# Smaller stages for the weight preparation at the seam between two stages of a fused attention and feed-forward kernel

## The chip, the cores and the metric

One core of one Trainium2 chip runs the whole kernel. The metric is device microseconds (us) of one execution; the kernel before took 1059.97 us (median of three runs, 1059.31 to 1060.24). The engines are PE (matmuls and weight loads), DVE (vector), ACT (scalar), POOL (GpSimd) and SP, whose queue issues the DMAs. Each engine works through its own list of instructions in order; semaphores hold an instruction until its inputs are there.

## The reference

Attention over 4 x 8 heads of 576 tokens and 64 dimensions, with scores below the row's maximum minus `tau` masked out, and then two feed-forward layers over the 2304 tokens:

```python
x = attention(q, k, v, tau)          # [2304, 512]
h = ((x @ w1) * (x @ w2)) @ w3       # gated, d_ff 1024
h3 = h @ w_out                       # [2304, 512]
g = h3 @ w_in                        # second layer, d_ff 2048
out = np.maximum(0.01 * g, g) @ w2_out
```

All of it is wanted in float32 accuracy; the weights arrive as 64-bit numbers.

## The kernel before

**Numbers.** A float32 matrix is held as a high part that PE can take (`fp32r`) and a low part, the rest; a product is then three matmuls (high x high, high x low, low x high, the table `PASSES`). The 64-bit weights come from HBM as pairs of 32-bit words into a tile `st`. `words` turns one `st` into two integer tiles `t` and `lw` with two ACT conversions (L640, L641) and a DVE shift of `t` (L642); a POOL addition of `t` and `lw` makes the float32 (L657 for up weights, L691 for down weights). `t` and `lw` have two buffers each, `st` has four.

**Stages.** Attention runs first, with the gated layer of each group of tokens as filler between its steps (`gated`: eight parts i; each has 24 `psab` matmuls on PE (L439), a copy `at` on ACT (L445), the product of the two halves on DVE (L447), a cast of `gt` to its high part on ACT (L449) and a subtraction for the low part on POOL (L450). Four outputs o follow, each of 24 `psh` matmuls (L458) that take the eight `gt` in order, a copy `ht` (L465) and a store to `h3d`). The gated layer of the last group has no attention left beside it: it is the chain `last`, walked step by step. Beside it run `first_h3`, which builds the operands `h3` of the second layer, and the first weight preparations; the table `early` says at which steps.

**The second layer** takes the tokens in three chunks of 768 and d_ff in eight quadruples (`NQ`), so 24 products n. `products(n)` is seven blocks of six matmuls (L854; a scheme with seven products of half-size blocks) into two banks of PSUM in turn; each block's bank is freed by a copy `snap` on ACT (L831), a `sum` on DVE (L836) or the activation `gf` on ACT (L841). `down(n)` is 36 `po` matmuls (L889); five follow each block of the next product and six the last.

**The preparations.** `prepare_up(q)` makes the seven combinations of quadruple q (`full`: one L664 and three L711 on DVE), their high parts `uph` (two ACT casts of 768 and 1024 columns, L671) and low parts `upl` (two DVE subtractions, L674), and stores both to `up_d` (L677) for the later chunks. `prepare_down(q)` makes `dn`: per half a cast (L690) and a subtraction (L711), then a store to `dn_d` (L695). In the first chunk, product n calls one step of `prepare_up(n + 2)` per block and, from block 3, one of `prepare_down(n + 1)`; what is left runs after block 6. `fetch` brings a quadruple's tiles back in the later chunks; for three of eight they are still in place. `load_h3` prepares the next chunk's operands during the last product of a chunk. ACT, DVE and POOL take their instructions in the order in which the code issues them (`manual_schedule`); so does PE.

Of the kernel before, what the change touches and what calls it, by code (L numbers as in the profile page):

```python
# [43 lines left out]
def attention_gated_ffn(ctx: ExitStack, tc: tile.TileContext, qkv, tau, w3t, wout, w12, w2, out):  # L44
# [576 lines left out]
    ups = [[(q + NQ, 0), (q, 0)] for q in range(NQ)] + [[], []]  # L621
    downs = [[(q, 1), (q + NQ, 1)] for q in range(NQ)]
    order = ups[0] + downs[0] + ups[1] + [x for q in range(1, NQ + 1) for x in ups[q + 1] + downs[q % NQ]][:-2]
# [9 lines left out]
    def words(j, c):  # L633
# [7 lines left out]
        nc.scalar.activation(lw, low.bitcast(U32), AF.Copy, scale=2.0 ** -29)  # L641
        nc.vector.tensor_scalar(out=t, in0=t, scalar1=3, scalar2=None, op0=ALU.logical_shift_left)  # L642
        used[0] += 1
        return t, lw

    def prepare_up(q):
# [3 lines left out]

        full = wpool.tile([P, 8, HF], F32, tag=tag(q), name="full")
        uph, upl = up_tiles(q)
        kept = None
        for j, part in ((q + NQ, full[:, 0:2]), (q, full[:, 2:4]), (None, None)):
            if kept:
                into, t, lw = kept
                nc.gpsimd.tensor_tensor(  # L657
                    out=into.rearrange("p a w -> p (a w)").bitcast(I32), in0=t, in1=lw, op=ALU.add)
            if j is not None:
                kept = (part, *words(j, 0))  # L660
                issue()
            yield
# [7 lines left out]
        for lo, hi in parts:  # L670
            nc.scalar.copy(uph[:, lo:hi], full[:, 1 + lo:1 + hi])  # L671
        yield
# [3 lines left out]
        for i, part in enumerate((uph, upl)):  # L676
            nc.sync.dma_start(out=up_d[q, i], in_=f(part.rearrange("p a w -> p (a w)")))  # L677
        yield

    def prepare_down(q):  # L680

        dn = down_tile(q)
        kept, low = None, None
        for i in range(4):
            if low is not None:
                less(dn[:, i - 2, 1], f(low), f(dn[:, i - 2, 0]))
                low = None
            if kept:
                t, low = kept
                nc.scalar.copy(dn[:, i - 1, 0], f(t))  # L690
                nc.gpsimd.tensor_tensor(out=low, in0=t, in1=low, op=ALU.add)  # L691
            kept = words(q + i * NQ, 1) if i < 2 else None
            issue()
            if i == 3:
                nc.sync.dma_start(out=dn_d[q], in_=f(dn.rearrange("p a b w -> p (a b w)")))  # L695
            yield
# [276 lines left out]
```

## Time and profile before

| | |
|---|---|
| median of three runs | 1059.97 us |
| profiled execution | 1061.28 us, span 1059.5 us |
| PE busy | 1027.7 us (97%) |
| DVE, ACT, POOL busy | 582.3, 547.2, 282.5 us |
| chain that ended last, by engine | PE 90%, ACT 4%, DVE 3%, POOL 1%, issue 1% |
| mean granted clock of PE | 0.987 |

The times of a row are of one profiled execution, whose own time stands above; its span runs from the first to the last instruction. A row of an engine's timeline gives start, duration, line, operation, output and inputs, the number of instructions merged into it, and in brackets the idle time before it with what ended that. The granted clock of PE has two levels, 1.00 (2.4 GHz) and 0.50 (1.2 GHz); a mean over a stretch lies between.

### The profile page before, as it was taken

How to read it: one execution, taken by the hardware profiler on the slowest of the kernel's cores; microseconds unless marked ns; L12 is line 12 of the kernel's file. 1: busy time of each engine (PE TensorE's matmuls, PEld its weight loads, DVE VectorE, ACT ScalarE, POOL GpSimd, SP SyncE). 2: the span in 40 equal slices, each digit the busy share in tenths (PEclk: the TensorE clock that was granted, in tenths of full speed). 3: DMA queues.
4: the chain of work that ended last, by engine and by line, in shares of the span. 5: the costliest groups of instructions: out<-in, count | busy, mean ns of one | idle time of the engine just before them, and what ended most of it. 6: DMA issues, size and time to landing. Idle time of an engine off the chain costs nothing.

```text
span 1059.5 us, 17342 instructions
## 1 busy us (share of the span) xinstructions
PE 1027.7 (97%) x6632; PEld 885.3 (84%) x6632; DVE 582.3 (55%) x1269; ACT 547.2 (52%) x1052; POOL 282.5 (27%) x299
## 2 busy tenths in 40 slices
PE   7999799999999999999999997899999999999998
PEld 6554488889988989988998996899999999999997
DVE  7757867665676566776657646367663111621111
ACT  5767755444454444554545435578855333542332
POOL 3536712021211120211111236244442111411110
PEclk9999899999999999999999998899999999999999
DMA  9644321312121212121210226588955443045301
GB/s 310 241 166 153 116 59 40 102 37 66 42 58 51 61 37 77 30 61 50 60 39 26 80 61 243 209 302 312 378 194 189 166 167 144 1 138 215 149 1 60
DMA packets 42467, 129.58 MB, mean 122 GB/s; under 512 B 5520, under 2 KB 20880, under 8 KB 38032
## 3 DMA queue, kind: packets, MB, share of 16 engines
q1 hardware_dynamic: 42240, 128.47, 35.1%
q8 instruction: 52, 0.85, 0.3%
q14 instruction: 31, 0.25, 0.1%
q10 hardware_dynamic: 144, 0.00, 0.0%
HBM read 95.95 MB, written 32.51 MB: 121 GB/s over the span
## 4 chain that ended last, share of the span: by engine, by line
PE 90%; ACT 4%; DVE 3%; POOL 1%; issue 1%; DMA 0%; SPq 0%; POOLq 0%; ACTq 0%; DVEq 0%
PE psab L439 19%; PE po L889 19%; PE ps L854 17%; PE psh L458 10%; PE av L338 7%; PE sc L262 7%; PE tp L316 5%; PE ps L405 3%; PE tq L321 1%; DVE t L152 1%; ACT t L149 1%; PE bc L368 1%; PE tp L305 1%; ACT e L271 1%; PE scratch L510 1%
## 5 line engine op out<-in xcount | busy, mean ns | idle before, releaser
L439 PE MATMUL psab<-x,w 128*128 128x256 f32 (+1 forms) x1536 | 231.9, 302 | 0.0
L889 PE MATMUL po<-dn,gg 128*128 128x512 f32 x864 | 224.2, 392 | 0.0
L439 PEld LDWEIGHTS psab<-x,w 128*128 128x128 f32 x1536 | 208.7, 189 | 13.5 <-issue 9.5
L889 PEld LDWEIGHTS po<-dn,gg 128*128 128x128 f32 x864 | 161.0, 188 | 22.3
L854 PE MATMUL ps<-h,uph 128*128 128x384 f32 x672 | 174.7, 341 | 2.7 <-DVE sum L836 2.7
L271 ACT ACTIVATE e<-sc,nm 128x576 f32<-128x576 f32 x144 | 102.5, 741 | 89.3 <-DVE nm L269 89.2
L269 DVE TENSOR_REDUCE nm<-sc 128x1 f32<-128x576 f32 x144 | 103.2, 752 | 78.1 <-PE sc L262 78.1
L854 PEld LDWEIGHTS ps<-h,uph 128*128 128x128 f32 x672 | 124.7, 189 | 17.2 <-DVE sum L836 3.8
L458 PE MATMUL psh<-gt,w 128*128 128x256 f32 (+1 forms) x768 | 119.5, 307 | 7.1 <-ACT gt L449 5.8
L836 DVE TENSOR_TENSOR sum<-snap,ps 128x384 f32<-128x384 f32 x72 | 39.7, 551 | 154.4 <-PE ps L854 149.6
L450 POOL TENSOR_TENSOR gt<-at,gt 128x256 fp32r<-128x256 f32 (+1 forms) x64 | 51.8, 810 | 270.3 <-ACT gt L449 270.1
L285 DVE SCALAR_TENSOR_TENSOR e<-sc,th,e 128x576 f32<-128x576 f32 x144 | 113.8, 814 | 11.6 <-ACT e L271 11.2
L458 PEld LDWEIGHTS psh<-gt,w 128*128 128x128 f32 x768 | 106.8, 193 | 13.7 <-ACT gt L449 6.8
L854 PE MATMUL ps<-h,upl 128*128 128x384 f32 x336 | 114.2, 340 | 0.0
L844 POOL TENSOR_TENSOR gg<-sum,gg 128x384 fp32r<-128x384 f32 x48 | 48.9, 1019 | 224.7 <-ACT gg L843 201.6
L316 PE MATMUL tp<-ident,e 128*128 128x128 f32 x512 | 77.3, 274 | 12.2 <-ACT HH L320 12.2
L831 ACT COPY snap<-ps 128x384 f32<-128x384 f32 x72 | 34.5, 480 | 103.5 <-PE ps L854 103.4
L316 PEld LDWEIGHTS tp<-ident,e 128*128 128x128 f32 x512 | 60.6, 140 | 21.9 <-ACT HH L320 14.7
L318 DVE COPY HH<-tp 128x512 f32<-128x512 f32 x64 | 44.0, 688 | 48.2 <-PE tp L316 47.4
L338 PE MATMUL av<-HH,vv 128*64 128x256 f32 (+1 forms) x512 | 67.5, 406 | 0.0
L854 PEld LDWEIGHTS ps<-h,upl 128*128 128x128 f32 x336 | 63.6, 189 | 0.0
L405 PE MATMUL ps<-wo,w 128*128 128x512 f32 x128 | 60.3, 616 | 3.3 <-DVE xs L369 3.3
(124 smaller groups left out, 1402.6 us busy)
## 6 DMA issues: line engine op xcount, KB each, us to landing
st<-in_w SPq DMA_DIRECT2D x40, 512.0 KB, 5.1
vv<-in_qkv SPq DMA_DIRECT2D x64, 160.0 KB, 2.3
dn<-dn_d SPq DMA_DIRECT2D x10, 1024.0 KB, 6.9
uph<-up_d SPq DMA_DIRECT2D x10, 896.0 KB, 8.0
upl<-up_d SPq DMA_DIRECT2D x10, 896.0 KB, 4.7
raw<-in_w3t SPq DMA_DIRECT2D x8, 1024.0 KB, 6.4
dn_d<-dn SPq DMA_DIRECT2D x8, 1024.0 KB, 7.1
up_d<-uph SPq DMA_DIRECT2D x8, 896.0 KB, 4.9
```

The source lines that it names most:

```text
L262: nc.tensor.matmul(sc[a][:, half, :HS], lhs, rhs, start=(i == 0), stop=(i == len(passes) - 1))
L269: nc.vector.tensor_reduce(out=nm, in_=sc[a][:, :, :HS], op=ALU.max, axis=AX.XY, negate=True)
L271: nc.scalar.activation(e[a].rearrange("p (a b) -> p a b", a=2), sc[a][:, :, :HS], AF.Exp, bias=nm)
L285: nc.vector.scalar_tensor_tensor(out=ev, in0=sc[a][:, :, :HS], scalar=th, in1=ev, op0=ALU.is_ge, op1=ALU.mult, accum_out=stat[key][:, o:o ...
L316: nc.tensor.transpose(tp[:, kc], e[a][:, kc * P:kc * P + P], ident)
L338: nc.tensor.matmul(av[a * D:a * D + D, :gw], vv[:, a, kc], rhs, start=(i == 0), stop=(i == NK - 1))
L405: nc.tensor.matmul(ps, w3_t[i][:, j * P:j * P + P], wo_t[j // 2][:, (j % 2) * 512:(j % 2) * 512 + 512], start=(j == 0), stop=(j == KF - 1))
L439: nc.tensor.matmul(ps[:, :gw], w12_t[i][:, a, mat * 512 + kk * P:mat * 512 + kk * P + P], xt[kk][:, c, :gw], start=(m == 0), stop=(m == 11))
L450: nc.gpsimd.tensor_tensor(out=gt[i][:, 1, :gw], in0=at[:, :gw], in1=f(gt[i][:, 0, :gw]), op=ALU.subtract)
L458: nc.tensor.matmul(ps[:, :gw], w34_t[i // 2][:, a, i % 2, o * P:o * P + P], gt[i][:, c, :gw], start=(m == 0), stop=(m == 23))
L854: nc.tensor.matmul(ps, (uph, upl)[a][:, wi, i * P:i * P + P], hs[k][:, c, i], start=(opens[k] and m == 0), stop=(m == 5), skip_group_check ...
L889: nc.tensor.matmul(po_t[o], gg[:, c, t * P:t * P + P], dn[:, i, a], start=(q == 0 and seen[o] == 1 and m == 0), stop=(q == NQ - 1 and seen ...
```

## The change

Six things move; what is computed stays.

- `prepare_up` has eight steps instead of five: both pairs of conversions, each shift, each POOL addition, the combinations, the casts with the store of `uph`, and the two `upl` subtractions, the second with its store. `prepare_down` has five instead of four.
- The shift of `t` leaves `words` for a function of its own and is issued one step after the conversions; the next load is issued inside `words`.
- Beside the last gated stage `prepare_up(0)` takes steps 10 to 17 (9 to 14 before), `prepare_up(1)` 16 to 23 (16 to 21) and `prepare_down(0)` 20 to 24 (12 to 15). Step 24 lies in the `psh` matmuls of output 2.
- In the products, `prepare_up(n + 2)` begins in block 5 of product n and runs on into product n + 1. `prepare_down(n)` begins in block 1 of product n itself; before, that work was done in product n - 1. The last one, of quadruple 7, begins in block 5 of product 6 and ends in product 7.
- `order`, the sequence of loads, follows.
- `fetch` of a tile that is still in place is called at its own product; `load_h3` takes its `t2` tiles two steps later.

```diff
-    early = [(start, 1, 9), (prepare_up(0), 9, 14), (prepare_down(0), 12, 15), (prepare_up(1), 16, 21)]
+    early = [(start, 1, 9), (prepare_up(0), 10, 17), (prepare_up(1), 16, 23), (prepare_down(0), 20, 24)]
...
     def words(j, c):
...
-        nc.vector.tensor_scalar(out=t, in0=t, scalar1=3, scalar2=None, op0=ALU.logical_shift_left)
         used[0] += 1
+        issue()
         return t, lw
+
+    def shift(t):
+        nc.vector.tensor_scalar(out=t, in0=t, scalar1=3, scalar2=None, op0=ALU.logical_shift_left)
...
     def prepare_up(q):
+        t1, lw1 = words(q + NQ, 0)
+        yield
+        t2, lw2 = words(q, 0)
+        shift(t1)
+        yield
         full = wpool.tile([P, 8, HF], F32, tag=tag(q), name="full")
         uph, upl = up_tiles(q)
...
+        nc.gpsimd.tensor_tensor(out=whole[:, :512], in0=t1, in1=lw1, op=ALU.add)
+        shift(t2)
+        yield
+        nc.gpsimd.tensor_tensor(out=whole[:, 512:1024], in0=t2, in1=lw2, op=ALU.add)
+        yield
...
+        nc.sync.dma_start(out=up_d[q, 0], in_=f(uph.rearrange("p a w -> p (a w)")))
         yield
         for lo, hi in parts:
             nc.vector.tensor_tensor(
                 out=upl[:, lo:hi], in0=full[:, 1 + lo:1 + hi], in1=f(uph[:, lo:hi]), op=ALU.subtract)
-        for i, part in enumerate((uph, upl)):
-            nc.sync.dma_start(out=up_d[q, i], in_=f(part.rearrange("p a w -> p (a w)")))
-        yield
+            if lo:
+                nc.sync.dma_start(out=up_d[q, 1], in_=f(upl.rearrange("p a w -> p (a w)")))
+            yield
...
     def prepare_down(q):
...
+        for i in range(5):
+            if i > 2:
+                less(dn[:, i - 3, 1], f(ts[i - 3][1]), f(dn[:, i - 3, 0]))
+            if 1 < i < 4:
+                t, lw = ts[i - 2]
+                nc.scalar.copy(dn[:, i - 2, 0], f(t))
+                nc.gpsimd.tensor_tensor(out=lw, in0=t, in1=lw, op=ALU.add)
+            if i < 2:
+                ts.append(words(q + i * NQ, 1))
+            if 0 < i < 3:
+                shift(ts[i - 1][0])
+            if i == 4:
                 nc.sync.dma_start(out=dn_d[q], in_=f(dn.rearrange("p a b w -> p (a b w)")))
             yield
...
     for n in range(total):
         ci, q = divmod(n, NQ)
-        if n + 2 >= NQ and n + 2 < total:
-            fetch(n + 2)
-        works = [prepare_up(n + 2) if n + 2 < NQ else iter(()), prepare_down(n + 1) if n + 1 < NQ else iter(())]
+        for ahead_by in (0, 2):
+            m = n + ahead_by
+            if NQ <= m < total and (m % NQ < 3) == (ahead_by == 0):
+                fetch(m)
         for k, _ in enumerate(products(n)):
             run(prior, 5 if k < 6 else 36)
-            run(works[0], 1)
-            if k > 2:
-                run(works[1], 1)
+            if k == 5 and n + 2 < NQ:
+                steps.append(prepare_up(n + 2))
+            if (k == 1 and 0 < n < NQ - 1) or (k == 5 and n == NQ - 2):
+                steps.append(prepare_down(n + k // 5))
+            for one in steps:
+                run(one, 1)
```

**The order it makes.** Three places, all on DVE. The first is the end of the last gated stage, from the combinations of quadruple 0 on; `at` (L447) is the product that `gt` waits for. Before:

```order
L664 TENSOR_TENSOR full<-full 128x256
L711 TENSOR_TENSOR full<-full 128x256 x3
L642 TENSOR_SCALAR t<-t 128x512 x2
L447 TENSOR_TENSOR at<-psab,at 128x320
L674 TENSOR_TENSOR upl<-full,uph 128x768
L674 TENSOR_TENSOR upl<-full,uph 128x1024
L711 TENSOR_TENSOR dn<-lw,dn 128x512 x2
L447 TENSOR_TENSOR at<-psab,at 128x320
L642 TENSOR_SCALAR t<-t 128x512 x2
L447 TENSOR_TENSOR at<-psab,at 128x320
```

and now:

```order
L447 TENSOR_TENSOR at<-psab,at 128x320
L668 TENSOR_TENSOR full<-full 128x256
L718 TENSOR_TENSOR full<-full 128x256 x3
L447 TENSOR_TENSOR at<-psab,at 128x320
L679 TENSOR_TENSOR upl<-full,uph 128x768
L679 TENSOR_TENSOR upl<-full,uph 128x1024
L645 TENSOR_SCALAR t<-t 128x512
L447 TENSOR_TENSOR at<-psab,at 128x320
L645 TENSOR_SCALAR t<-t 128x512
L668 TENSOR_TENSOR full<-full 128x256
```

Before, three products of parts 5, 6 and 7 stood after the combinations; now two do (parts 6 and 7), and both `dn` subtractions and the second quadruple's shift are gone from in front of the last.

The second place is product 0, from the first `sum` to the last `gg`. Before:

```order
L642 TENSOR_SCALAR t<-t 128x512
L836 TENSOR_TENSOR sum<-snap,ps_8052 128x384
L642 TENSOR_SCALAR t<-t 128x512
L664 TENSOR_TENSOR full<-full 128x256
L711 TENSOR_TENSOR full<-full 128x256 x3
L642 TENSOR_SCALAR t<-t 128x512
L836 TENSOR_TENSOR sum<-snap,ps_8051 128x384
L642 TENSOR_SCALAR t<-t 128x512
L836 TENSOR_TENSOR sum<-snap,ps_8052 128x384
L844 TENSOR_TENSOR gg<-sum,gg 128x384
```

and now:

```order
L843 TENSOR_TENSOR sum<-snap,ps_8052 128x384
L843 TENSOR_TENSOR sum<-snap,ps_8051 128x384
L843 TENSOR_TENSOR sum<-snap,ps_8052 128x384
L851 TENSOR_TENSOR gg<-sum,gg 128x384
L851 TENSOR_TENSOR gg<-gf,gg 128x384
L645 TENSOR_SCALAR t<-t 128x512 x2
```

No shift and no combination stands between the three `sum` any more; the two shifts for quadruple 2 come after them.

The third is the beginning of product 7, where `h3` of the next chunk is prepared (`h` and `h3r`). Before:

```order
L711 TENSOR_TENSOR dn<-lw,dn 128x512
L844 TENSOR_TENSOR gg<-gf,gg 128x384
L711 TENSOR_TENSOR dn<-lw,dn 128x512
L723 TENSOR_TENSOR h_9131<-h3r,h_9131 128x384
L836 TENSOR_TENSOR sum<-snap,ps_9117 128x384
L723 TENSOR_TENSOR h_9149<-h3r,h_9149 128x384
L711 TENSOR_TENSOR h3r<-h3r 128x384
```

and now:

```order
L645 TENSOR_SCALAR t<-t 128x512 x2
L730 TENSOR_TENSOR h_9124<-h3r,h_9124 128x384
L843 TENSOR_TENSOR sum<-snap,ps_9107 128x384
L718 TENSOR_TENSOR dn<-lw,dn 128x512
L730 TENSOR_TENSOR h_9145<-h3r,h_9145 128x384
L718 TENSOR_TENSOR dn<-lw,dn 128x512
L718 TENSOR_TENSOR h3r<-h3r 128x384
```

The two `dn` subtractions of quadruple 7 have moved from ahead of the first `h` to behind the product's first `sum`, in front of the work on `h3r`.

## Rows read from the trace of the kernel before

**Rows 1.** Busy us by stretch: PE, PEld, DVE, ACT, POOL; then clock, DMA share, GB/s.

```profile
640.00:700.00 60.00, 50.13 (x257) 45.55 (x256) 32.34 (x51) 36.07 (x67) 25.07 (x22) 0.86 0.69 250
750.00:800.00 50.00, 50.00 (x252) 45.50 (x251) 33.79 (x52) 34.35 (x70) 22.99 (x20) 1.00 0.69 260
```

**Rows 2.** Timeline of PE, 19 to 24 us and the seam: start, us, instructions, idle before.

```profile
21.88 0.66 PE L316 MATMUL tp<-ident,e 128*128 128x128 f32 x4 [2.38 <-ACT HH L320]
...
620.14 28.32 PE L439 MATMUL psab<-x,w 128*128 128x320 f32 x192
648.30 2.36 PE L458 MATMUL psh<-gt,w 128*128 128x320 f32 x15
...
656.16 0.64 PE L458 MATMUL psh<-gt,w 128*128 128x320 f32 x1 [3.68 <-ACT gt L449]
...
660.95 13.44 PE L458 MATMUL psh<-gt,w 128*128 128x320 f32 x74 [0.30 <-POOL gt L450]
...
683.95 1.01 PE L854 MATMUL ps<-h,uph 128*128 128x384 f32 x2 [2.68 <-DVE sum L836]
```

**Rows 3.** Instructions on the tile `at` from 618 to 662 us, and who waited.

```profile
L449 ACT CAST gt<-at x8: 457/459/463, 630.5 to 659.5; 128x320 fp32r<-128x320 f32 x8
L450 POOL TENSOR_TENSOR gt<-at,gt x8: 860/880/1068, 631.0 to 660.0; 128x320 fp32r<-128x320 f32 x8
...
  PE psh L458: 7.1, 6
```

**Rows 4.** Timeline of DVE in the last gated stage.

```profile
645.35 1.89 DVE L711 TENSOR_TENSOR full<-full 128x256 f32<-128x256 f32 x3
...
650.19 2.75 DVE L674 TENSOR_TENSOR upl<-full,uph 128x768 fp32r<-128x768 f32 x2
652.87 2.35 DVE L711 TENSOR_TENSOR dn<-lw,dn 128x512 fp32r<-128x512 f32 x2
655.14 0.48 DVE L447 TENSOR_TENSOR at<-psab,at 128x320 f32<-128x320 f32 x1
...
664.49 1.23 DVE L674 TENSOR_TENSOR upl<-full,uph 128x1024 fp32r<-128x1024 f32 x1 [0.24 <-ACT uph L671]
```

**Rows 5.** Chain that ended last, at 690 us.

```profile
690.43 1.06 PE ps L854 x6
691.49 1.13 PE po L889 x5
```

**Rows 6.** Timeline of ACT in the last gated stage.

```profile
638.79 0.42 ACT L445 COPY at<-psab 128x320 f32<-128x320 f32 x1
639.11 0.67 ACT L640 ACTIVATE t<-st 128x512 f32<-128x512 f32 x1
639.68 0.65 ACT L641 ACTIVATE lw<-st 128x512 int32<-128x512 uint32 x1
...
647.27 1.06 ACT L671 CAST uph<-full 128x1024 fp32r<-128x1024 f32 x1 [1.08 <-DVE full L711]
```

**Rows 7.** Timeline of POOL, same stage.

```profile
642.40 2.74 POOL L657 TENSOR_TENSOR full<-t,lw 128x512 int32<-128x512 int32 x2
...
651.82 2.24 POOL L691 TENSOR_TENSOR lw<-t,lw 128x512 int32<-128x512 int32 x1
```

**Rows 8.** Granted clock by stretch (columns as in rows 1), after three waits.

```profile
21.00:24.40 3.40, 2.52 (x21) 2.40 (x23) 3.33 (x9) 3.17 (x7) 1.60 (x2) 1.00 0.99 375
662.70:666.10 3.40, 3.40 (x14) 3.40 (x14) 2.74 (x4) 1.39 (x2) 0.00 (x0) 0.50 0.41 163
683.10:686.50 3.40, 2.53 (x7) 2.03 (x8) 1.68 (x4) 3.34 (x6) 1.80 (x2) 0.51 0.69 267
```

**Rows 9.** DMA issues from 740 to 800 us: KB each, us to landing.

```profile
st<-in_w SPq DMA_DIRECT2D x5, 512.0 KB, 7.8
```

**Rows 10.** Timeline of all engines in product 7.

```profile
793.71 0.54 DVE L836 TENSOR_TENSOR sum<-snap,ps 128x384 f32<-128x384 f32 x1
...
794.71 0.52 PE L854 MATMUL ps<-h,uph 128*128 128x384 f32 x2
```

More of the change, by code (lines that the diff above doesn't have):

```diff
@@ L619, in down_tile @@
         return quads[n][2]
-    ups = [[(q + NQ, 0), (q, 0)] for q in range(NQ)] + [[], []]
-    downs = [[(q, 1), (q + NQ, 1)] for q in range(NQ)]
-    order = ups[0] + downs[0] + ups[1] + [x for q in range(1, NQ + 1) for x in ups[q + 1] + downs[q % NQ]][:-2]
+    order = [(q + i * NQ, c) for n in range(-1, NQ) for q, c in ((n + 1, 0), (n, 1)) if 0 <= q < NQ for i in ((0, 1) if c else (1, 0))]
     raws, used = [], [0]
@@ L641, in words @@
         nc.scalar.activation(lw, low.bitcast(U32), AF.Copy, scale=2.0 ** -29)
+        used[0] += 1
+        issue()
+        return t, lw
+    def shift(t):
         nc.vector.tensor_scalar(out=t, in0=t, scalar1=3, scalar2=None, op0=ALU.logical_shift_left)
-        used[0] += 1
-        return t, lw
     def prepare_up(q):
+        t1, lw1 = words(q + NQ, 0)
[3 more added lines that the diff above has]
+        yield
         full = wpool.tile([P, 8, HF], F32, tag=tag(q), name="full")
         uph, upl = up_tiles(q)
[L653 to L661, printed above, removed]
-            yield
+        whole = full.rearrange("p a w -> p (a w)").bitcast(I32)
+        nc.gpsimd.tensor_tensor(out=whole[:, :512], in0=t1, in1=lw1, op=ALU.add)
[3 more added lines that the diff above has]
+        yield
         a21, a22, a11, a12 = (full[:, i] for i in range(4))
@@ L675, in prepare_up @@
                 out=upl[:, lo:hi], in0=full[:, 1 + lo:1 + hi], in1=f(uph[:, lo:hi]), op=ALU.subtract)
-        for i, part in enumerate((uph, upl)):
-            nc.sync.dma_start(out=up_d[q, i], in_=f(part.rearrange("p a w -> p (a w)")))
-        yield
+            if lo:
+                nc.sync.dma_start(out=up_d[q, 1], in_=f(upl.rearrange("p a w -> p (a w)")))
+            yield
     def prepare_down(q):
         dn = down_tile(q)
[L683 to L694, printed above, removed]
+        ts = []
+        for i in range(5):
[10 more added lines that the diff above has]
+            if i == 4:
                 nc.sync.dma_start(out=dn_d[q], in_=f(dn.rearrange("p a b w -> p (a b w)")))
@@ L777, in load_h3 @@
         b12, b22 = ([raw[o + i][:, TW:2 * TW] for i in range(2)] for o in (0, 2))
-        t2 = [f(wld.tile([P, 512], I32, tag="t", name="t2", bufs=2))[:, :TW] for _ in range(2)]
         slots = h3_t[ci] = []
@@ L789, in load_h3 @@
         yield
+        t2 = [f(wld.tile([P, 512], I32, tag="t", name="t2", bufs=2))[:, :TW] for _ in range(2)]
         for i in range(2):
@@ L920, in attention_gated_ffn @@
             run(ahead, 1)
-        for _ in chain(*works):
-            pass
         prior = down(n)
```

1 line of the change is left out of this document (added).

## The prediction

> **What bounds the kernel now.** I read the stages first [rows 1]: for each stretch the busy time of every engine, and the granted clock of the matrix engine (PE). From 750 to 800 us PE is busy 50.00 of 50.00 us at clock 1.00: nothing done by the other engines can help there. The loss is at the seam: from 640 to 700 us PE is busy 50.13 of 60.00, at clock 0.86. So the second reading was PE's own order of time there [rows 2]. The 192 matmuls of the last gated part (`psab`) run without a gap from 620.14 to 648.30, 0.147 us each. Then the 96 `psh` matmuls need the eight `gt` tiles, and the last 74 of them start only at 660.95; and one block of the first product waits 2.68 us for a DVE `sum`, at 683.95. The view of the tile `at` [rows 3] says who is late: PE waits 7.1 us in six waits for `gt`. DVE's order [rows 4] shows why: the L447 of 655.14 stands behind two `upl` subtractions (2.75 us) and two `dn` subtractions (2.35 us), with a ready operand. It is the preparation of the weights, queued ahead of what PE waits for, that is bound to be the loss; PE is the bound elsewhere.
>
> How much is there to win? From 648.30 to 690.43, where the second block of product 1 starts [rows 2, 5], lie 42.13 us. At full clock their content is 96 matmuls of 0.147 (14.08), eight blocks of six matmuls at 1.06 (8.48) and five `po` matmuls, 1.13: 23.69. The rest, 18.4 us, is the most the change can give at this place: waits, and half clock after them.
>
> **The change, part by part.** No arithmetic on the weights is added or removed: the same casts, shifts, adds, subtractions and DMA bytes, in another order. PE's order is the same. So the working is a walk through the new order, with the durations of the trace.
>
> *The last gated parts.* I start where both orders agree: the `at` copy of part 3 ends at 639.21 [rows 6]. Per part: `at` copy 0.42 [rows 6], DVE product 0.48 [rows 4], ACT cast 0.46 and POOL subtraction 0.88 [rows 3]; a pair of word conversions holds ACT 1.14 (starts 0.57 apart [rows 6]). Part 3's cast now goes before the first pair: cast 640.0, pair 640.4, part 4's `at` 641.5, second pair 641.8, part 4's cast 643.0, part 5's `at` 643.3, its cast 644.3. POOL does part 4 from 643.5 to 644.3, then the two word additions, 2.74 together [rows 7], to 647.05, then part 5 to 648.0, in time for PE (needed at 650.7). DVE's four combinations end 2.1 us after the second addition, as now (645.14 to 647.24 [rows 7, 4]): 649.15. Part 6's product stands behind them, though its `at` was ready at 645.1: it ends at 649.6. ACT casts `uph` in two pieces (the second one 1.06 [rows 6]) to 650.25, then part 6 to 650.65. Both `upl` pieces then hold DVE, the second (1.23 alone [rows 4]) from its cast on, to about 651.6.
>
> Here a row and a page meet. POOL's addition at 651.82 took 2.24 us [rows 7] where two others took 2.74 together, and it ran beside DVE's `upl` and `dn` subtractions. So I let POOL's part 6 wait until the second `upl` piece is done, and put it at 651.6 to 652.45. If POOL did not wait it would be done by 651.6, and the sum would be some 0.8 us better. The Trainium skill ("SBUF — State Buffer", SBUF: two separate sides) has the first as a rule: GpSimd and a DVE instruction with two SBUF inputs exclude each other for a whole instruction; by it the sum stays as it is.
>
> Part 7: the pair of conversions for quadruple 1 and part 7's `at` end at 652.1; DVE's shift, which I let wait for POOL too, ends at 652.75, the product ends at 653.25; a second pair keeps ACT until 653.2; cast to 653.75, POOL to 654.65. PE would want it at 651.5. So PE starts the last 74 `psh` matmuls at 654.7 instead of 660.95, after some 3.2 us of waiting in three pieces. They would end at 654.7 + 10.85 = 665.55 at full clock (674.38 now).
>
> *Product 0.* The conversions for quadruple 2 and both `dn` subtractions no longer stand between the `sum` instructions: preparation of quadruple 1 and of the first down weights ends by my walk at about 664.5, before the product starts. A `sum` needs 0.55 and has a block of 1.06 us to be in time, so I cost the stall of 2.68 us at nothing; its bound from above is what it is now. One pair (1.14 on ACT) is placed in block 5, ahead of the cast that frees PE's bank for block 1 of product 1; by my walk that is just in time, without margin, and costs at most one pair. Seven blocks, block 0 of product 1 and five `po`: 665.55 + 7.42 + 1.06 + 1.13 = 675.16 against 690.43. **15.27 us** sooner.
>
> *The clock.* Half clock cost 2.5 us after the first wait (74 matmuls in 13.44 instead of 10.85 [rows 2]). The granted clock was 0.50 (1.2 GHz, the lower of its two levels) in a stretch after it that PE filled, and 0.51 after the wait of 2.68 us, while after a wait of 2.38 us, at 21.88 [rows 2], it stood at 1.00, 2.4 GHz [rows 8]. The new wait of 3.2 us, with a few matmuls in it, is longer than both, so I take one fall at the row of the same matmuls: **2.5 us back**; the ends are nothing and 3.2, what the second fall cost (two blocks and five `po` from 683.95 to 690.43, 6.48 instead of 3.25 [rows 2, 5]).
>
> A page can be read against that: the Trainium skill ("TensorE: Matmul & The Clock Gate", What's actually happening) gives the lower clock to an engine that has been idle, and there are matmuls between the pieces of my wait. If they keep it up, no fall comes and the sum is 2.5 us better. The trace does not show which it is: where it has a wait broken up in this way, before 660.95, one unbroken wait of 3.68 us is among the six [rows 2]. So this is a rival.
>
> *The quadruples after.* Per quadruple seven blocks and 36 `po` take 15.6 us; PE has no idle time there [rows 1]. Walking product 1 through the new order, ACT and DVE free each bank 2 us or more before PE wants it (the copy for block 0 of product 2 some 2.8), so I cost that at nothing; the cover is this margin. On SP's queue the `uph` store goes ahead of the word loads and the `upl` store follows a step later; loads stay three ahead of use, some 11 us, and land after 7.8 [rows 9]. `fetch` for the tiles that are kept issues no transfer.
>
> *The hand-over.* The down weights of quadruple 7 are now finished inside product 7, where the next chunk's `h3` is prepared. There the `sum` at 793.71 ends at 794.25, and PE's block 6 starts at 794.71 [rows 10]: a margin of 0.46. Two `dn` subtractions now stand before it; two took 2.35 beside a POOL addition [rows 4], perhaps 1.0 to 1.4 without it. So PE waits 0.5 to 1.9 us, more or less as POOL and the later `h3` loads fall. I take **1.0 us**, with 0 and 3.5 as ends: the last `h3` load is behind the last word conversion now and can hold up ACT.
>
> **The sum.** 15.3 − 2.5 − 1.0 = 11.8 us. The profiled execution took 1061.28 us in all, for a span of 1059.5, which is 1.3 above the median; a difference carries over, so 1059.97 − 11.8 = **1048.2 us**.
>
> **The rivals.**
> - *The wait is too short for the clock to fall, or smaller than I walked.* For it: the case at 21.88, and the matmuls inside the wait. Against: the fall after the shorter wait at 683.95. Time: 2.5 less, 1045.7; with no wait left at all, 15.3 + 3.2 − 1.0 = 17.5 better, 1042.5.
> - *More small waits than I see*: a longer half clock (3.2), the hand-over at 3.5, a pair of conversions too many at product 1 (1.1): 4.3 worse than forecast, 1052.5 together, 1050 to 1052 for two of them. For it: margins of 0.0 and 0.46.
> - *The spreading does not spread*: the last gated part comes as late as now (660.95), because four combinations and two `upl` still stand ahead of L447. Then only product 0 wins: from 674.38 to 690.43 are 16.05 us with 9.61 of content, so 6.4, less 1.0: 1054.5. Against: the `dn` subtractions and one `upl` pair do leave the place.
> - *Slower: ACT becomes the bound in the quadruples.* Two conversions now stand on ACT at a product's end, ahead of the copy that frees a bank for the next. If each of the seven seams waits like the `sum` at 683.95 (2.68), that is 18.8 − 11.8 = 7 us slower, 1067; it decides from 2 us at each. Against: by my walk ACT would have to be 4 us later than it is.
>
> **How the numbers follow.** Forecast 0.50, shorter wait 0.22, more small waits 0.16, no spreading 0.08, slower 0.04. A measurement of this kernel tells about 0.2%, 2.1 us, from no change; all but the last case are beyond it, with a little for the border: faster 0.94, same 0.02, slower 0.04. For 8 in 10 the range leaves out the slower and the no-spreading case (0.12) and, with a few hundredths each, the wait that vanishes and all small waits at once: 1043.3 to 1052.0.
>
> **What would show it.** Right: the last run of 74 `psh` starts near 654.7; no wait for `sum` in product 0; one stretch at 0.50 after 651; a DVE `sum` wait of about 1 us in product 7. Wrong: `psh` starting at 651 or at 660; clock 1.00 throughout the seam; PE idle in products 1 to 6, above all a wait for ACT's `snap` or `gf`.

## The result and the profile after

The changed kernel takes **1049.72 us** (median of four runs, 1048.59 to 1052.29), against 1059.64 for the kernel before beside it: a ratio of 0.991, 95% interval 0.9891 to 0.993. That is 9.9 us faster; 11.8 were forecast, and 1049.72 lies 1.5 us above the forecast of 1048.2.

The profiled execution of the changed kernel is the fastest of the four (1048.59 us, span 1046.8, mean granted clock 0.995). The others stand at 1049.62, 1049.83 and 1052.29 us with clocks of 0.993, 0.993 and 0.992. So the trace probably shows an execution with less half clock than the rest.

The stages of the changed kernel, columns as in [rows 1]:

```profile
640.00:700.00 60.00, 57.78 (x329) 54.05 (x328) 38.71 (x60) 43.53 (x84) 29.83 (x23) 1.00 0.75 273
750.00:800.00 50.00, 46.71 (x232) 41.62 (x231) 29.19 (x48) 30.83 (x64) 23.01 (x19) 1.00 0.67 251
```

The seam has gone from 50.13 to 57.78 busy of 60.00 us and from clock 0.86 to 1.00. But the second stretch, which PE filled, now has a hole of 3.29 us. PE's timeline shows both places, with the idle time in brackets:

```profile
646.80 2.95 PE L458 MATMUL psh<-gt,w 128*128 128x320 f32 x19
650.70 0.55 PE L458 MATMUL psh<-gt,w 128*128 128x320 f32 x2 [0.94 <-POOL gt L450]
651.93 0.42 PE L458 MATMUL psh<-gt,w 128*128 128x320 f32 x1 [0.69 <-ACT gt L449]
652.94 11.12 PE L458 MATMUL psh<-gt,w 128*128 128x320 f32 x74 [0.59 <-POOL gt L450]
...
673.59 0.61 PE L861 MATMUL ps<-h,uph 128*128 128x384 f32 x2
...
776.37 0.62 PE L861 MATMUL ps<-h,uph 128*128 128x384 f32 x2 [2.43 <-ACT snap L838]
...
781.90 0.62 PE L861 MATMUL ps<-h,uph 128*128 128x384 f32 x2 [0.86 <-DVE sum L843]
```

Compare with [rows 2]. The 74 matmuls start 6.14 us after the first `psh` instead of 12.65, and take 11.12 us instead of 13.44. Product 0 has no wait. The second block of product 1 (673.59) comes 26.79 us after the first `psh`; before it was 41.96 by the same view (690.26), so the seam gave 15.17 us. `psh` itself began 1.50 us sooner in this execution, for nothing that the change touches: in the traces of all versions it begins between 645.63 and 648.30. From the second block of product 1 to the end of PE's last matmul (673.59 to 1043.20; 690.26 to 1055.90 before) the changed kernel needs 3.97 us more: the two waits of 3.29 in product 7, and 0.7 that lies in no wait. 15.17 + 1.50 - 3.97 is the 12.7 between the two profiled executions.

What held PE in product 7 is a transfer, and both waits go back to it, as the chain that ended last shows there:

```profile
766.26 0.02 ACT snap L838
...
766.34 9.05 DMA h3r<-h3d
...
776.01 1.39 POOL h L730
...
777.43 1.37 DVE h3r L718
778.79 2.59 DVE h L730 x2
781.38 0.48 DVE sum L843
```

ACT's timeline shows why PE cares:

```profile
765.36 0.67 ACT L639 ACTIVATE lw<-st 128x512 int32<-128x512 uint32 x1
...
775.42 0.51 ACT L729 CAST h<-h3r 128x384 fp32r<-128x384 f32 x1 [6.39 <-DMA h3r<-h3d]
775.84 0.47 ACT L838 COPY snap<-ps 128x384 f32<-128x384 f32 x1
```

and SP's queue why the load is late:

```profile
764.85 1.40 SPq L714 DMA_DIRECT2D uph<-up_d  x1
766.34 1.21 SPq L781 DMA_DIRECT2D h3r<-h3d  x1
```

The last `h3r` load takes the `st` buffer of the last word conversion (over at 766.03), so SP issues it at 766.34, right behind a fetch of 896 KB. It lands 9.05 us later. ACT's cast of it stands ahead of the `snap` copy that frees PE's bank. The later wait for `sum` (0.86) is at block 6, the place that the prediction named, but its chain runs from the same load over POOL's `h` and DVE's `h3r` and `h`.

### The profile page after: what moved, and what is told of

It reads as the page before. It is cut to its first block, busy times and chain, and to the rows that moved or that the text cites. A ratio compares the mean times of both kernels' runs of the same rounds, so it can differ in the third digit from the quotient of the medians.

```text
span 1046.8 us, 17373 instructions
## 1 busy us (share of the span) xinstructions
PE 1020.3 (97%) x6632; PEld 879.1 (84%) x6632; DVE 579.3 (55%) x1269; ACT 546.8 (52%) x1052; POOL 288.2 (28%) x299
## 4 chain that ended last, share of the span: by engine, by line
PE 88%; ACT 4%; DVE 3%; DMA 2%; issue 2%; POOL 1%; SPq 0%; POOLq 0%; ACTq 0%; DVEq 0%
PE po L896 18%; PE psab L439 17%; PE ps L861 17%; PE psh L458 10%; PE av L338 7%; PE sc L262 7%; PE tp L316 5%; PE ps L405 3%; PE tq L321 1%; DMA h3r<-h3d 1%; DVE t L152 1%; ACT e L271 1%; ACT t L149 1%; PE tp L305 1%; PE bc L368 1%
## 5 line engine op out<-in xcount | busy, mean ns | idle before, releaser
L851 POOL TENSOR_TENSOR gg<-sum,gg 128x384 fp32r<-128x384 f32 x48 | 51.5, 1073 | 250.0 <-ACT gg L850 231.0
L458 PE MATMUL psh<-gt,w 128*128 128x256 f32 (+1 forms) x768 | 115.5, 302 | 2.2 <-POOL gt L450 1.5
L458 PEld LDWEIGHTS psh<-gt,w 128*128 128x128 f32 x768 | 104.0, 189 | 7.7 <-issue 3.5
L848 ACT ACTIVATE sum<-sum 128x384 f32<-128x384 f32 x72 | 37.9, 526 | 49.6 <-DVE sum L843 49.6
```

Source lines behind the costliest of these rows:

```text
L458: nc.tensor.matmul(ps[:, :gw], w34_t[i // 2][:, a, i % 2, o * P:o * P + P], gt[i][:, c, :gw], start=(m == 0), stop=(m == 23))
```

## The experiments

All ratios are to the kernel before, run on the same chip beside them. "The mark" is the time from the first `psh` matmul to the second block of product 1, in the profiled execution: 41.96 us before, 26.79 after the change.

### The change in two parts

The first run keeps the new stages everywhere, but puts the old places back in the loop.

```diff
-            if k == 5 and n + 2 < NQ:
+            if k == 0 and n + 2 < NQ:
                 steps.append(prepare_up(n + 2))
-            if (k == 1 and 0 < n < NQ - 1) or (k == 5 and n == NQ - 2):
-                steps.append(prepare_down(n + k // 5))
+            if k == 3 and n + 1 < NQ:
+                steps.append(prepare_down(n + 1))
...
+        for _ in chain(*steps):
+            pass
```

> The new stages and the new order at the seam, but inside the products the old places: up weights of quadruple n+2 from block 0 of product n, down weights of n+1 from its block 3, all finished by the product's end. Theory (the seam gives the gain, the later down weights give the loss): the last 74 psh matmuls start about 6.1 us after the first psh matmul as in the changed kernel (12.65 before); product 7 has no wait (the last h3 load starts a quadruple-block or more sooner), so 3.3 us come back. If product 0 can carry the work of quadruple 2 and of down weights 1 as well, the second block of product 1 starts 26 to 28 us after the first psh and the kernel takes 1046 to 1047. Rival (the old places in the loop were what stalled product 0): the sum of product 0 is late again by up to 2.7 us with half clock behind it, 30 to 34 us at that mark, 1050 to 1054.

Measured: 1059.13 us, ratio 0.9995 (0.9986 to 1.0003), no gain at all and slower than either expectation. The 74 matmuls do start 6.2 us after the first `psh`, and product 7 has no wait at all. But product 0 waits 3.0 us for a `sum`, product 1 1.1 for the activation `gf` on ACT and 1.2 for a `sum`, and each of products 2 to 6 1.0 for a `sum`. The mark stands at 34.45. PE's timeline in product 2:

```profile
703.87 0.62 PE L861 MATMUL ps<-h,uph 128*128 128x384 f32 x2 [1.06 <-DVE sum L843]
```

and DVE's before it:

```profile
698.96 2.05 DVE L679 TENSOR_TENSOR upl<-full,uph 128x768 fp32r<-128x768 f32 x1
700.93 0.68 DVE L718 TENSOR_TENSOR dn<-lw,dn 128x512 fp32r<-128x512 f32 x1
701.54 1.21 DVE L679 TENSOR_TENSOR upl<-full,uph 128x1024 fp32r<-128x1024 f32 x1
702.67 0.68 DVE L718 TENSOR_TENSOR dn<-lw,dn 128x512 fp32r<-128x512 f32 x1
703.27 0.54 DVE L843 TENSOR_TENSOR sum<-snap,ps 128x384 f32<-128x384 f32 x1
```

The finer stages, put in the old places, bring four subtractions together ahead of one `sum`. Then the mirror image, the kernel before with the new places in the loop:

```diff
-            run(works[0], 1)
-            if k > 2:
-                run(works[1], 1)
+            if k == 5 and n + 2 < NQ:
+                steps.append(prepare_up(n + 2))
+            if (k == 1 and 0 < n < NQ - 1) or (k == 5 and n == NQ - 2):
+                steps.append(prepare_down(n + k // 5))
+            for one in steps:
+                run(one, 1)
...
-        for _ in chain(*works):
-            pass
```

> The old stages and the old order at the seam (word conversions, additions and casts in the stages of the kernel before), but the new places inside the products: up weights from block 5, down weights from block 1 of their own product. Theory: the last 74 psh matmuls start 12 to 13 us after the first as before; product 0 holds less preparation, so its 2.68 us wait and the half clock behind go (6.4 us), and product 7 waits 2 to 3.5 us for the last h3 load: 1055 to 1057.5. Rival (the stall of product 0 comes from the seam's backlog, not from the loop): the stall stays and only the hand-over's loss is added: 1062 to 1063.5.

Measured: 1066.67 us, ratio 1.0068 (1.0055 to 1.0081): slower than either expectation. Product 0 has no wait, as its theory said, but each of products 1 to 6 waits 1.2 us for a `sum`, and product 7 2.53 for `snap`. So stages and places are one edit; neither half of it can be judged with the other's partner. A fair division is by quadruple: the new stages and places for quadruples 0 and 1 and the first down weights, the old ones (`old_up`, `old_down`, as before) from quadruple 2 on.

```diff
+        works = [old_up(n + 2) if n + 2 < NQ else iter(()), old_down(n + 1) if n + 1 < NQ else iter(())]
...
-            for one in steps:
-                run(one, 1)
+            run(works[0], 1)
+            if k > 2:
+                run(works[1], 1)
...
```

> One part alone: quadruples 0 and 1 and the first down weights by the new stages and in the new places at the seam; from quadruple 2 on the old stages in the old places (a quadruple's up weights from block 0, down weights from block 3, as before). In the earlier run the new stages in the old places made a wait of 1.0 us for sum in every product. Theory: that came of the new stages meeting the old places, so here products 1 to 6 have no wait, as before, and product 7 has none either; the last 74 psh matmuls start 6.1 us after the first as in the changed kernel, 6.5 sooner than before, with 1.5 to 2.5 us of half clock in some runs. What is left open is product 0, which again carries two conversions of quadruple 2 and two of down weights 1: if its 2.68 us wait came of the seam's lateness it goes, 1046 to 1047.5; if it came of the old places it stays, with half clock behind, 1050 to 1053. Rival to all: the old places need 1 us per product whatever stands at the seam: 1056 to 1059.

And the other way round:

```diff
-    early = [(start, 1, 9), (prepare_up(0), 10, 17), (prepare_up(1), 16, 23), (prepare_down(0), 20, 24)]
+    early = [(start, 1, 9), (old_up(0), 9, 14), (old_down(0), 12, 15), (old_up(1), 16, 21)]
```

> The other part alone: old stages and old places at the seam (quadruples 0 and 1, down weights 0), from quadruple 2 on the new stages in the new places. Theory: the psh wait and the half clock behind it are those of before (74 matmuls start 12 to 13 us after the first), products 1 to 6 have no wait, product 0 has none or under 1 us because quadruple 2 starts only in block 5, and product 7 has the 2 to 3.5 us of the changed kernel: 6.4 less 3.3 better than before, 1056 to 1057.5. Rival (the seam's lateness makes product 0 wait, not its own work): the 2.68 us stay, 1060 to 1063.

Measured: the new seam alone 1052.54 us, 0.9933 (0.992 to 0.9945); the new loop alone 1057.88, 0.9983 (0.9974 to 0.9992). The first lies in the range that was given for a stall from the old places, the second 0.4 us above its theory's range. That is 7.3 and 2.0 us better than before (1059.86), together 9.3 of the 9.9: the parts add, within the intervals. PE's waits, first in the run with the new seam, from 652 to 690 us:

```profile
652.97 12.65 PE L458 MATMUL psh<-gt,w 128*128 128x320 f32 x74 [0.60 <-POOL gt L450]
675.19 1.01 PE L922 MATMUL ps<-h,uph 128*128 128x384 f32 x2 [2.68 <-DVE sum L904]
```

and DVE's list ahead of that `sum`, with the combinations of quadruple 2, which waited for POOL's addition:

```profile
673.11 1.22 DVE L779 TENSOR_TENSOR full<-full 128x256 f32<-128x256 f32 x3 [2.84 <-POOL full L725]
674.25 0.42 DVE L711 TENSOR_SCALAR t<-t 128x512 int32<-128x512 int32 x1
674.59 0.55 DVE L904 TENSOR_TENSOR sum<-snap,ps 128x384 f32<-128x384 f32 x1
```

then in the run with the new loop, DVE in product 0, where the `sum` waits for nothing but PE,

```profile
677.81 0.56 DVE L905 TENSOR_TENSOR sum<-snap,ps 128x384 f32<-128x384 f32 x1 [2.59 <-PE ps L923]
```

and PE in product 7:

```profile
785.26 0.61 PE L923 MATMUL ps<-h,uph 128*128 128x384 f32 x2 [2.92 <-ACT snap L900]
```

The stall of product 0 stays at 2.68 us with the seam's work over on DVE 12 us earlier (662.89), and goes with the new loop although the seam is as late as before. It comes from the work of quadruple 2 and down weights 1 inside product 0, not from a backlog. The hand-over's loss belongs to the loop alone: PE waits 2.92 us here and not at all in the run with the new seam, which needs 365.68 us from the second block of product 1 to the end (365.64 before, 369.61 in the changed kernel).

### The waits at the seam

Two runs take the preparation away from in front of the last gated parts. The first holds the combinations of quadruple 0 for two steps, the second for four; quadruple 1 and down weights 0 follow two steps later in both. The edit is that of the second; the first has two `yield` and 19 for 21.

```diff
+        for _ in range(4 if q == 0 else 0):
+            yield
         a21, a22, a11, a12 = (full[:, i] for i in range(4))
...
-    early = [(start, 1, 9), (prepare_up(0), 10, 17), (prepare_up(1), 16, 23), (prepare_down(0), 20, 24)]
+    early = [(start, 1, 9), (prepare_up(0), 10, 21), (prepare_up(1), 18, 25), (prepare_down(0), 22, 26)]
```

> The changed kernel, where the four combinations, uph casts and upl subtractions of quadruple 0 and all of quadruple 1 and down weights 0 come two steps later, behind the subtraction and cast of the last two gated parts. Theory (what stands ahead of the last two parts on DVE and ACT is all that makes PE wait at the seam, and the wait brings the half clock that comes in some runs): the three waits, 2.2 us, fall to 0 to 0.7, the 74 matmuls start 4 to 4.7 us after the first and take 11.1 in every run, mean clock 0.995 or more in all runs; the median is 2.2 plus the mean half clock (about 1.1) better than the changed kernel, 1046 to 1047.5, and the runs lie closer together. Rival (the preparation then ends too late): product 0 or 1 waits for uph or a sum, 1 to 3 us, and the time is 1047.5 to 1050. The hand-over's 3.3 us stay in both.

> As the run with the gates first, but the four combinations of quadruple 0 two steps later again, so that nothing of the preparation but the two word additions stands ahead of any of the gated parts on DVE, ACT and POOL; there they still stood ahead of the last part's product and PE waited 1.27 us. Theory (that order is the whole cause of the waits at the seam): no wait for gt is left, 0 to 0.3 us; the 96 psh matmuls run in 14.1 to 14.5 from the first on, the 74 start 3.2 to 3.6 after the first; no half clock between 640 and 700 us, whichever run; 2.2 us and the seam's half clock better than the changed kernel: 1045.5 to 1047.5. Rival (uph and upl of quadruple 0, now cast after the gates, are late for product 0): a wait of 0.5 to 2 us at the first product block in place of the old ones, 1047 to 1049.

Measured: with two steps 1047.86 us, 0.9887 (0.9871 to 0.9903); with four 1046.34, 0.9875 (0.9862 to 0.9889). PE's timeline, first with two steps, then with four:

```profile
645.63 3.42 PE L458 MATMUL psh<-gt,w 128*128 128x320 f32 x22
650.32 11.12 PE L458 MATMUL psh<-gt,w 128*128 128x320 f32 x74 [1.27 <-POOL gt L450]
```

```profile
646.93 14.24 PE L458 MATMUL psh<-gt,w 128*128 128x320 f32 x96
```

With two steps the combinations still stood ahead of the last part's product, and one wait of 1.27 us was left, more than the 0 to 0.7 that was expected; with four there is none, and the time lies in its theory's range. Without waits the mark is 23.77 us, and the content of this stretch was worked out as 23.69: nothing is left to win there. No wait came up in product 0 or 1 instead, so the rival falls in both. The part of the first expectation on the scatter was wrong: with two steps the executions lie from 1045.72 to 1050.01, with four from 1045.55 to 1048.33. Both versions keep the hand-over's waits.

### The hand-over

Four runs look at the 3.29 us in product 7. First, down weights 6 and 7 one block sooner in product 6; second, the last of the four `h3` loads in two tiles of its own (the ones for the output copies, idle then), with all orders on DVE, ACT and POOL kept:

```diff
-            if (k == 1 and 0 < n < NQ - 1) or (k == 5 and n == NQ - 2):
-                steps.append(prepare_down(n + k // 5))
+            if 0 < n < NQ - 1 and k == (1 if n < NQ - 2 else 0):
+                steps.append(prepare_down(n))
+            if n == NQ - 2 and k == 4:
+                steps.append(prepare_down(n + 1))
```

```diff
-        for o in range(KD):
+        for o in range(KD - 1):
...
+        two = [p2.tile([P, DM], F32, tag="os", name="h3o", bufs=3)[:, :TW] for _ in range(2)]
+        for i in range(2):
+            c = ci * 2 * TW + i * TW
+            nc.sync.dma_start(out=two[i], in_=h3d[KD - 1, :, c:c + TW])
```

> The changed kernel with the preparation of down weights 6 and 7 one block (2.2 us) sooner in product 6, so that the buffer of the last word conversion, which the last h3 load of the next chunk takes, comes free one block sooner, and this load stands ahead of the upl store and of the uph prefetch in SP's queue. Theory (the waits of 2.43 and 0.86 us in product 7 come from the last h3 load, which landed 9.1 us after its issue): the load lands 4 to 6 us sooner, before 772, and both waits go, 3 us better than the changed kernel, about 1046.5. Rival (the dn subtractions on DVE ahead of sum are the cause): they move by one block too, so the wait shrinks or stays near 1 us; and ACT carries two conversions nearer to the bank-freeing copies of product 6: 0 to 1.5 us better, 1048 to 1049.5, waits left in product 6 or 7.

> The changed kernel, where only the last of the four h3 loads has another buffer: two 128x384 tiles of the output copies, idle then, so that it waits for no word conversion and is issued long before. Places and order of all work on DVE, ACT and POOL stay. Theory (the load is the cause): the 6.39 us of ACT waiting for it go, the wait of 2.43 us on snap goes, and with it most of the 0.86 us on sum: 2.4 to 3.3 us better than the changed kernel, 1046.4 to 1047.3. Rival (the dn subtractions on DVE and the shared port with POOL are the cause): at least 1.5 to 3.3 us of waiting stays in product 7, and the time stays at 1048.2 to 1049.7.

Measured: 1048.95 us, 0.99 (0.9886 to 0.9913), and 1048.14, 0.9887 (0.9872 to 0.9902). ACT's wait for the load is 1.15 us in the first and gone in the second. Yet PE still waits 2.05 and 2.35 us for the same `snap`. ACT in the run with the own buffer:

```profile
770.18 0.51 ACT L729 CAST h<-h3o 128x384 fp32r<-128x384 f32 x1
...
775.96 0.52 ACT L729 CAST h<-t 128x384 fp32r<-128x384 f32 x1 [2.60 <-DVE t L718]
778.79 0.51 ACT L729 CAST h<-t 128x384 fp32r<-128x384 f32 x1 [2.32 <-DVE t L718]
779.21 0.47 ACT L843 COPY snap<-ps 128x384 f32<-128x384 f32 x1
```

Behind the load stood a second cause that ended almost as late: the same cast-before-`snap` order on ACT, now waiting for DVE's subtractions. The load's wait shrank or went, as the theories said, but the times came out as the rivals had them (the second's 0.06 us below its range). The next two runs keep the own buffer and move the `h3` work: first the first cast to the end of product 6 and the eight subtractions one block ahead of the casts; then also the casts one block later, behind the `snap` copy.

```diff
             less(b21[i], b21[i], t2[i])
+        yield
+        yield
         for src in (t2, b11, b12, b22, b21):
...
             ahead = load_h3(ci + 1)
-            run(ahead, 1)
+            run(ahead, 2)
...
-            if q == NQ - 1:
+            if q in (0, NQ - 1):
                 run(ahead, 1)
```

The earlier of the two has one `yield` and the old condition.

> The changed kernel with the last h3 load in a buffer of its own, as in the earlier run, and the first two steps of the h3 preparation half a block to a block sooner: the first cast at the end of product 6, and the eight subtractions one block ahead of the casts that read them. In the earlier run with the own buffer PE still waited 2.35 us, because ACT's cast of the subtracted tile stood ahead of the snap copy and waited 2.32 us for DVE. Theory (with the load gone the bound is this order on ACT, not DVE's sum of work): the cast no longer waits, the 2.35 us go to 0 to 0.6, 3 us better than the changed kernel: 1046 to 1047. Rival (DVE is full from 771 to 782 us, two dn subtractions and eight of h3 beside POOL): the wait moves to sum in block 1 or 4 and 1 to 2.3 us stay: 1047.3 to 1048.5.

> The changed kernel with the last h3 load in a buffer of its own, the first cast of h3 at the end of product 6, the eight subtractions in block 1, and now the casts that read them one block later than in the earlier split, in block 3, behind the snap copy; the last cast then falls into block 0 of product 8. Theory (what PE waited for was ACT's in-order queue: the snap copy stood behind a cast that waited 2.3 to 2.4 us for DVE): product 7 has no wait, or under 0.5 us, no half clock at 770 to 790 us, and 3.3 us come back against the changed kernel: 1045.7 to 1047. Rival (DVE's sum of work is the bound, two dn subtractions and eight of h3 stretched beside POOL): the wait moves to the sum of block 4 or 5 and 1 to 2.3 us stay: 1047.5 to 1049.

Measured: 1049.87 us, 0.9909 (0.9893 to 0.9924), with 1.90 us of wait for `snap` left, so no gain, slower than either expectation; and 1048.73, 0.9888 (0.9872 to 0.9904). In the second the wait for `snap` is gone, and another stands in its place. PE's timeline:

```profile
782.45 0.62 PE L868 MATMUL ps<-h,uph 128*128 128x384 f32 x2 [1.27 <-DVE sum L850]
```

and DVE's before it:

```profile
773.91 1.32 DVE L718 TENSOR_TENSOR dn<-lw,dn 128x512 fp32r<-128x512 f32 x1
...
780.77 0.69 DVE L718 TENSOR_TENSOR dn<-lw,dn 128x512 fp32r<-128x512 f32 x1
781.37 0.55 DVE L730 TENSOR_TENSOR h<-t,h 128x384 fp32r<-128x384 f32 x1
781.84 0.55 DVE L850 TENSOR_TENSOR sum<-snap,ps 128x384 f32<-128x384 f32 x1
```

DVE works from 769.72 to 784.15 with no gap of over 0.2 us. So the order on ACT was the cause of the `snap` wait, as the theory has it, and the rival has the new wait's place and size. (The times alone do not show the gain: the executions of these four runs scatter by 2.2 to 4.0 us, and their intervals overlap that of the changed kernel. The waits of the traces are the better measure.)

### Both together, and the last 1.27 us

The four steps' hold at the seam and the later casts together:

> Both edits together, the gates first and the h3 casts later. Theory (the two places are independent): the gains add, 2.2 to 3.3 at the seam with its clock and 2.4 to 3.3 in product 7: 1042.5 to 1045, with no wait of PE of over 0.3 us between 640 us and the end of product 8 and clock 1.00 there. Rival (half clock comes anyway in the start-up and the rest of a gain is lost in noise of the start): 1045 to 1047.

Measured: **1043.5 us** (1043.03 to 1043.78), ratio 0.9845 (0.9832 to 0.9859): 6.2 us better than the changed kernel, 16 better than before, inside the theory's range. PE has one wait of over 0.25 us after 640 us, which the theory did not expect:

```profile
646.52 14.24 PE L458 MATMUL psh<-gt,w 128*128 128x320 f32 x96
...
776.30 0.61 PE L870 MATMUL ps<-h,uph 128*128 128x384 f32 x2 [1.27 <-DVE sum L852]
```

The last run takes both `dn` subtractions of quadruple 7 out of that stretch, to ahead of product 7's first `sum`, by starting down weights 6 and 7 in blocks 0 and 3 of product 6.

> The version with both edits, and down weights 6 and 7 one and two blocks sooner in product 6, so that no dn subtraction stands on DVE between the first and the second sum of product 7; there were two there (1.32 and 0.69 us). Theory (the 1.27 us wait for sum that is left in product 7 is the dn subtractions' own price, the term of the prediction put at 1.0): the second sum comes 1.3 to 2.0 us sooner, the wait is 0 to 0.2 us, and the time is about 1.2 us better than the version with both edits, 1042 to 1042.6. Rival (the eight h3 subtractions, stretched beside POOL, fill the gap by themselves, or ACT now carries two conversions too close to product 6's bank copies): 0.5 to 1.3 us of wait stays in product 7 or comes up in product 6: 1042.8 to 1044.

Measured: 1043.51 us, 0.9849 (0.9836 to 0.9863), no change. The `sum` behind the eight `h3` subtractions is in time now, but an earlier one in product 7 is late, by the same amount. PE's timeline:

```profile
770.06 0.61 PE L870 MATMUL ps<-h,uph 128*128 128x384 f32 x2 [1.27 <-DVE sum L852]
```

and DVE's before it:

```profile
764.57 1.79 DVE L720 TENSOR_TENSOR dn<-lw,dn 128x512 fp32r<-128x512 f32 x1
766.28 1.37 DVE L732 TENSOR_TENSOR h<-h3r,h 128x384 fp32r<-128x384 f32 x1
767.57 1.50 DVE L720 TENSOR_TENSOR dn<-lw,dn 128x512 fp32r<-128x512 f32 x1
768.99 0.55 DVE L732 TENSOR_TENSOR h<-h3r,h 128x384 fp32r<-128x384 f32 x1
769.46 0.54 DVE L852 TENSOR_TENSOR sum<-snap,ps 128x384 f32<-128x384 f32 x1
```

The theory falls, and the rival holds by its numbers but not by its reason: the wait is not at the eight `h3` subtractions, nor in product 6. What the two runs have in common is that two `dn` subtractions stand in this stretch of DVE, beside `h3` work that takes 1.3 to 1.4 us for some instructions and 0.55 for others of the same shape. Where the `dn` had been done in product 6, in the old places, no wait was left (the run with the new seam alone). That run differs in more than these two, so what the 1.27 us are made of is not shown. A version that does all of that work in product 6 with the new places was not tried: an earlier start of down weights 7 needs `t` and `lw` buffers that down weights 6 still hold.

## Why the prediction was right, and where not

**The last gated parts: right.** The walk had the 74 matmuls 6.4 us after the first `psh` (654.7 from 648.30); they came after 6.14, in three pieces as forecast, with 2.22 us of waiting. I had let POOL's subtraction for part 6 wait for the second `upl` piece. DVE's timeline of the changed kernel,

```profile
647.84 2.08 DVE L679 TENSOR_TENSOR upl<-full,uph 128x768 fp32r<-128x768 f32 x2
649.84 1.08 DVE L645 TENSOR_SCALAR t<-t 128x512 int32<-128x512 int32 x1
...
651.25 0.41 DVE L645 TENSOR_SCALAR t<-t 128x512 int32<-128x512 int32 x1
```

and POOL's

```profile
649.11 1.53 POOL L450 TENSOR_TENSOR gt<-at,gt 128x320 fp32r<-128x320 f32 x1 [2.66 <-ACT gt L449]
652.02 0.86 POOL L450 TENSOR_TENSOR gt<-at,gt 128x320 fp32r<-128x320 f32 x1 [1.38 <-ACT gt L449]
```

show both halves: POOL's took 1.53 us instead of 0.86 and ended 0.7 us after the `upl` pieces did (649.92), and the shift queued behind it took 1.08 instead of 0.41. The rule of the Trainium skill ("SBUF — State Buffer", SBUF: two separate sides), by which GpSimd and a DVE instruction with two SBUF inputs, or in a mode that uses two ports, exclude each other for a whole instruction, agrees with the `upl` row; in which mode the shift ran no run shows. The two runs that held the preparation back show the cause: take it from in front of the parts, and with two steps one wait of 1.27 us is left, with four none, and nothing in its place.

**Product 0: right, and for the right reason.** The work of quadruple 2 no longer stands between the `sum` instructions. The run with the new seam alone keeps the stall, the run with the new loop alone loses it.

**The walk's 15.27 us: right.** 15.17 in an execution without half clock.

**The clock: a certain 2.5 us back was the wrong form.** In the profiled execution the rival came true: clock 1.00 throughout the seam, one of the prediction's own signs of being wrong. (By its own row the term should also have been 2.6: 13.44 less 10.85.) In seven traces PE met this wait in three pieces, 1.9 to 2.2 us in all. Three ran the 74 matmuls in 11.12 us at clock 1.00, two in 12.65 (the run with down weights 7 sooner had clock 0.55 from 653.0 to 656.4, just after the wait), two in about 13.7, as with the old places in the loop:

```profile
652.83 13.70 PE L458 MATMUL psh<-gt,w 128*128 128x320 f32 x74 [0.37 <-POOL gt L450]
```

So the price is nothing, 1.5 or 2.6 us, and programs with the same order at the seam pay one or the other. That the slower executions of the changed kernel paid it is likely by their mean clock (0.992 and 0.993 against 0.995) but not shown, since only the fastest execution has a trace. The Trainium skill ("TensorE: Matmul & The Clock Gate", What's actually happening) says that the changes of clock fall differently from run to run of one kernel; the seven traces, one each of seven programs, fit that but do not test it. Some support is the version with both edits: its five executions lie within 0.75 us of each other, the changed kernel's four within 3.7. The four steps' hold alone, which still has the hand-over's waits, lies within 2.78.

**The quadruples: right as a result.** No wait in products 1 to 6. But the two runs with mixed stages and places waited 1.0 to 1.3 us in each of them, for DVE's `sum` and only once (1.1 us, for `gf` in product 1) for ACT, as my rival of the other side had it. The margin that I called a cover was not broad; it held for this order only. The runs do not show that rival's price of 2.68.

**The hand-over: the term that was mis-sized.** I took 1.0 us, for two `dn` subtractions ahead of a `sum`, and named the last `h3` load behind the last word conversion only for the upper end, 3.5. Measured are 3.29. The wait for `sum` at block 6, where I had looked, was 0.86, near my term by luck: its chain goes back to the load. With load and order on ACT out of the way 1.27 us stay there; that these are the `dn` subtractions' own price is not shown. Ahead of it stood what I had kept for the end: the load that ACT waited 6.39 us for, and behind it the order on ACT, a cast that waits for DVE ahead of the copy that PE waits for. They overlap: taking the load away won 0.94 us of the wait, taking the order away too another 1.08. The step that failed is the one where I looked for the wait on DVE's list and did not walk ACT's list and the load through product 7, though the rows of the DMA issues had a price near it: a median of 7.8 us for loads of 512 KB [rows 9].

**The sum.** 15.3 - 2.5 - 1.0 was forecast; in the profiled execution 15.2 - 0 - 4.0 came of it, 11.2, and the other executions gained 1 to 3.7 us less. A loss of clock that did not come and a hand-over that cost 2.3 us more than forecast in waits, and 0.7 outside them, met there with opposite signs. That the total came out near the forecast is in part luck; the walk of the seam is not.

## What to carry to other kernels

Where engines take their work in order, the stages of a background task and the places where its steps are called are one decision: with one moved without the other, this change lost all of its gain or became slower than before. Walk the list of every in-order engine through the stretch, also the one that is not late now, and ask of each instruction ahead of PE's releaser what it could wait for; behind a removed wait there stood twice another that ended about a microsecond sooner (0.94 and 1.08 us). A wait of PE cost more than its length only in some of the executions, so it is better to remove it than to shorten it, and the scatter of the times is a hint whether that is done: the last two versions, with one wait of 1.27 us left, lie within 0.75 and 0.26 us.

## What the runs showed of the hardware

- Waits of PE that look alike in the trace were followed by half clock in some executions and not in others. At the hand-over waits of 1.90, 2.05, 2.53, 2.92 and 3.21 us were followed by a stretch at half clock, and waits of 2.19, 2.35 and 2.43 were not; the length alone does not decide. What does is open.
- A 384 KB load took 3.2 us at best and 9.1 at worst from issue to landing in the changed kernel, the latter behind 2.8 MB of stores and a fetch that were issued within 3 us ahead of it, with the DMA share at 0.97 to 1.05 from 760 to 775 us. In the run with four steps' hold it took 10.0.
- The same DVE shift of 128x512 words took 0.41 us alone, 1.08 beside POOL at the seam, and 1.24 to 1.52 beside POOL at the hand-over in the last versions.
